# One TensorE run for a step's outputs, the next Gram products and the last transposes, in a scan with two feed-forward layers

## The chip, the cores and the metric

The kernel runs on one core of a Trainium2 chip. Its engines are TensorE (PE: matrix products and transposes; PEld is its loading of weights), VectorE (DVE), ScalarE (ACT), GpSimd (POOL) and SyncE (SP), whose queue issues most transfers (DMA). Each works through its own queue in order and waits at semaphores for the others. The metric is the device time of one execution in microseconds, as the median of several runs.

## What is computed

A chunked linear recurrence over 4 batches, 8 heads and 768 positions, then a normalisation and a gated layer, then a second layer with a squared ReLU:

```python
def _attn_ref(x, a, B, C):                 # head_dim 32, d_state 16
    log_a = np.log(np.clip(a, 1e-06, 1.0))
    for c in range(nc):                    # chunks of the sequence
        cum = np.cumsum(la, axis=-1)
        L = np.exp(cum[:, :, :, None] - cum[:, :, None, :]) * causal
        CB = np.einsum('bhin,bhjn->bhij', Cc, Bc)
        y_intra = np.einsum('bhij,bhjd->bhid', CB * L, xc)
        y_inter = np.einsum('bhin,bhnd->bhid', Cc, state) * np.exp(cum)[:, :, :, None]
        y[:, :, sl] = y_intra + y_inter
        state = decay_full[:, :, None, None] * state + np.sum(Bx, axis=2)

def _moe_ref(x, w_gate, w_val, w_out, rms_g):      # 3072 tokens, 256 -> 1536 -> 256
    xn = x / np.sqrt(np.mean(x * x, axis=-1, keepdims=True) + 1e-06) * rms_g
    g = xn @ w_gate
    return g * (1.0 / (1.0 + np.exp(-g))) * (xn @ w_val) @ w_out

def _moe2_ref(x, w_in, w_out, s, b):               # 256 -> 2048 -> 256
    r = np.maximum(x @ w_in, 0.0)
    return (s * (r * r) + b) @ w_out
```

## The kernel before

**The recurrence** is cut into 16 steps of 48 positions (counted from 0 here, as in the code). A step has two units, `c` and `c + 1`; each holds one chunk of two batches. In each step TensorE does three things for both units, all of them into the units' two PSUM tiles `y` (two banks each):

- `gram` (lines 549 to 565): 16 Gram products of B and C with a tile form of 32 rows by 64 columns (32*64 in the trace), read from `raw_bc`, which is loaded anew for each step by twelve transfers. From step 2 on this is the form used. DVE then multiplies them by the decays in `a_sb` to `m`, with four instructions.
- `outs` (586 to 617): 32 output products of `m` and `xh` in the form 64*64. `xh` holds the inputs of the chunk and, in 16 rows of each half, the state. ScalarE then copies the new state into the next step's `xh` (four copies), squares the rows for the norm and, after DVE (`ss`) and POOL (`rs`), scales them to `xn`.
- `turn` (637 to 658): 4 transposes of `xn`. ScalarE reads them from PSUM to `xth`, DVE writes the remainder to `xtl`. These are the columns of the first layer's input.

`scan` (495 to 504) comes before: it loads `a_sb` by two transfers (`load_a`), once the step before has used it, and a scan on DVE makes the decays.

**The layers** work on blocks of units, `BLOCKS = (4, 4, 4, 5, 5, 5, 5)`. For each of 12 hidden slices of a block, `hidden1` (774) has twelve products into the two banks `h`; ScalarE and DVE make `s`, `hi` and `lo` of them, and two slices later six products add to `o`. Each bank `h` is free for the next slice when ScalarE (first bank) and DVE (second bank, product `s`) have read it. The second layer follows when all steps are done, after some 322 us.

**What sets the order.** Nothing is issued where it is written. `Plan` records every instruction with its predecessors, plays the program through with costs of its own and issues all of it in the order that came out (line 370, which is why every row of the trace carries L370). The recorded order of the steps (`stream`, 661 to 669) sets what waits for what: an instruction that reads or overwrites a tile follows those recorded before it on that tile. `bundled` (507) makes the tile products of one kind and one step a group that the plan keeps together; `join` (131) gives the group's first instruction all waits of the others. Between the groups the plan puts products of the layers.

Of the kernel before, what the change touches and what calls it, by code (L numbers as in the profile page):

```python
# [8 lines left out]
F32 = mybir.dt.float32  # L9
# [10 lines left out]
P = 128  # L20
CH = 48
NST = 16
R = NST + CH
# [3 lines left out]
CPB = SEQ // CH  # L27
UT = 2 * CH
NPAIR = 2
NUNIT = CPB * NPAIR  # L30
NCLIP = 2 * NPAIR
FREE = 2 * NPAIR
SLOTS = NPAIR
AW = CH + 1
# [350 lines left out]
def scan_glu_relu2(ctx: ExitStack, tc: tile.TileContext, bc, xr, aa, cst, w1, w2, gn, sv, bv, out):  # L385
    nc = Plan(tc.nc)
# [19 lines left out]
    ps_y = ctx.enter_context(tc.tile_pool(name="ps_y", bufs=2, space=PS))  # L406
# [139 lines left out]
                            rhs=raw[:, 1:3, cols], start=True, stop=True, tile_position=(at, z * R),  # L546
                        )

    def gram(units):
        if units[0]:  # L550
            load_bc(units)
        for c in units:
            y_t[c] = ps_y.tile([P, 2, 512], F32, tag="y", name="y")
        bundled("g", units, gram_products, True)
        for c in units:
            g = gram_of(c)
            t = a_t.pop(c)
            m = att2.tile([P, NH, R], F32, tag="m", name="m")
            mv, tv = (v.rearrange("p (a b) r -> p a b r", a=2) for v in (m, t))
            nc.vector.tensor_tensor(out=mv[:, :, :, NST:R], in0=g[:, :, :, NST:R], in1=tv[:, :, :, 0:CH], op=ALU.mult)  # L560
            nc.vector.tensor_tensor(
                out=mv[:, :, :, 0:NST], in0=g[:, :, :, 0:NST],
                in1=tv[:, :, :, CH:AW].to_broadcast([P, 2, 4, NST]), op=ALU.mult,
            )
            m_t[c] = m
# [20 lines left out]
    def outs(units):  # L586
# [6 lines left out]
        if units[0] < FREE:  # L593
            nc.fresh = True
            for c in units:
                out_products([c])
                nc.fresh = True
        else:
            bundled("o", units, out_products, True)
        ss = att2.tile([P, NPAIR], F32, tag="ss", name="ss")  # L600
# [36 lines left out]
    def turn(units):  # L637
        for c in units:
            j = BLOCK[c]
            if c == FIRST[j]:  # L640
                xt_h[j] = xt_p.tile([P, 2, NB[j]], F32R if j else F32, tag="xth", name="xth")
                if j:
                    t = xt_p.tile([P, 2, NB[j]], F32R, tag="xtl", name="xtl")
                    xt_l[j] = [t[:, k] for k in range(2)]
        bundled("t", units, turn_products)
        for c in units:
            j, p = BLOCK[c], c % NPAIR
            step = steps_of(j, p).index(c // NPAIR)
            tp = y_t.pop(c)[:, 1, 4 * R:4 * R + 2 * P].rearrange("p (k z r) -> p k z r", k=2, z=2)
            src = [tp[:, k, :, NST:R] for k in range(2)]  # L650
            hi = [columns(xt_h[j][:, k], j, p)[:, step] for k in range(2)]
            for k in range(2):
                nc.scalar.activation(out=hi[k], in_=src[k], func=AF.Copy, scale=g_sb[:, k:k + 1])
            for k in range(2 if j else 0):
                lo = columns(xt_l[j][k], j, p)[:, step]
                nc.vector.scalar_tensor_tensor(
                    out=lo, in0=src[k], scalar=g_sb[:, k:k + 1], in1=f32(hi[k]), op0=ALU.mult, op1=ALU.subtract
                )


    def stream():
        s = []
        for c in range(0, NUNIT, NPAIR):
            units = range(c, c + NPAIR)
            s += [(6 * c + t, units, f) for t, f in zip((2, 4, 8), (scan, gram, outs))]
            apart = BLOCK[c] != BLOCK[c + 1]
            s += [(6 * c + 14, u, turn) for u in ([[c], [c + 1]] if apart else [units])]
        s.sort(key=lambda e: e[0])
        return [(units, f) for _, units, f in s]

# [494 lines left out]
```

## Time and profile before

| | |
|---|---|
| median of 3 runs | 630.87 us (630.2 to 632.45) |
| the profiled execution | 631.4 us |
| its span, first to last instruction | 629.4 us |
| TensorE busy | 619.1 us (98%) |
| VectorE busy | 481.7 us (77%) |
| ScalarE busy | 448.6 us (71%) |
| GpSimd busy | 49.4 us (8%) |
| granted TensorE clock | 0.999 of full speed |

The span stretches from the first to the last instruction of the program on any engine; the 2.0 us between it and the execution's time lie around it. A busy share is an average over stages. In a timeline of TensorE, a product starts before the one ahead of it has ended, since they are pipelined; the distance between two starts, not the duration of a row, tells what a product costs. An `xN` behind a row of the timeline counts trace records: each product of the small forms has two.

### The profile page before, as it was taken

What the parts mean: (1) busy time and instruction counts of PE and PEld (TensorE: products, weight loads), DVE (VectorE), ACT (ScalarE), POOL (GpSimd) and SP (SyncE); (2) the same over time, 40 slices, a digit from 0 to 9 for tenths busy, and PEclk for the clock granted to TensorE, in tenths of its full rate; (3) what the DMA queues carried; (4) which work ended last, traced back from release to release, by engine and by line L of the source; (5) the groups of instructions that cost most, each with busy time, mean ns of one, the idle gap of its engine ahead of it and who ended that gap; (6) DMA issues with size and microseconds to landing.
All of it is one profiled execution on the core that took longest, in us unless ns stands there. A gap on an engine that the chain in (4) does not pass through costs nothing.

```text
span 629.4 us, 12849 instructions
## 1 busy us (share of the span) xinstructions
PE 619.1 (98%) x4911; PEld 544.6 (87%) x4911; DVE 481.7 (77%) x972; ACT 448.6 (71%) x941; POOL 49.4 (8%) x88
## 2 busy tenths in 40 slices
PE   9899999999999999999999999999999999999996
PEld 7786899999888888888888889999999999999986
DVE  6999965778557656767774568798897897987976
ACT  5788635566545556664665579899898999998985
POOL 3000000001101111101232220000000000000000
PEclk9999999999999999999999999999999999999999
DMA  6877403344313433300200000001010010010101
GB/s 218 218 232 207 116 16 65 81 95 95 98 35 89 95 96 95 92 15 11 34 1 1 1 1 1 2 3 33 0 34 2 2 33 1 6 31 1 33 1 35
DMA packets 33694, 35.00 MB, mean 56 GB/s; under 512 B 14048, under 2 KB 30048, under 8 KB 33632
## 3 DMA queue, kind: packets, MB, share of 16 engines
q1 hardware_dynamic: 32688, 33.71, 20.7%
q8 instruction: 39, 0.64, 0.4%
q10 hardware_dynamic: 944, 0.46, 0.3%
q14 instruction: 23, 0.19, 0.1%
HBM read 30.90 MB, written 3.25 MB: 54 GB/s over the span
## 4 chain that ended last, share of the span: by engine, by line
PE 91%; DMA 2%; ACT 2%; DVE 2%; issue 1%; SPq 0%; DVEq 0%; ACTq 0%
PE h L370 52%; PE o L370 21%; PE acc L370 13%; PE y L370 5%; DMA a_sb<-a_scr 1%; DMA raw<-in_w 1%; PE o L363 1%; DVE a_sb L370 0%; ACT xth L370 0%; ACT e L370 0%; ACT xh L370 0%; DVE s L370 0%; ACT xn L370 0%; DVE m L370 0%; ACT sg L370 0%
## 5 line engine op out<-in xcount | busy, mean ns | idle before, releaser
L370 ACT CAST hi<-s 128x256 fp32r<-128x256 f32 (+2 forms) x170 | 80.1, 474 | 72.4 <-DVE s L370 69.9
L370 ACT ACTIVATE s<-h 128x512 f32<-128x512 f32 (+2 forms) x170 | 97.2, 572 | 36.1 <-PE h L370 33.1
L370 PE MATMUL h<-x1h,w2h 128*128 128x512 f32 x384 | 119.2, 391 | 0.0
L370 PE MATMUL h<-xth,w1h 128*128 128x480 f32 (+1 forms) x296 | 108.9, 371 | 1.4 <-DVE s L370 1.1
L370 PE MATMUL h<-xth,w1l 128*128 128x480 f32 (+1 forms) x296 | 109.3, 369 | 0.0
L370 PE MATMUL h<-xtl,w1h 128*128 128x480 f32 (+1 forms) x296 | 109.0, 370 | 0.0
L370 DVE TENSOR_TENSOR lo<-s,hi 128x256 fp32r<-128x256 f32 (+2 forms) x170 | 86.4, 509 | 28.1 <-ACT hi L370 25.4
L370 PE MATMUL acc<-hi,w2c 128*128 128x256 f32 x448 | 81.8, 281 | 0.0
L370 PEld LDWEIGHTS h<-x1h,w2h 128*128 128x128 f32 x384 | 69.2, 188 | 12.3
L370 DVE TENSOR_TENSOR s<-h,s 128x480 f32<-128x480 f32 (+1 forms) x74 | 45.6, 616 | 39.1 <-PE h L370 36.1
L370 PE MATMUL h<-x1l,w2h 128*128 128x512 f32 x192 | 75.0, 390 | 0.0
L370 PEld LDWEIGHTS acc<-hi,w2c 128*128 128x128 f32 x448 | 71.0, 189 | 2.3
L370 DVE TENSOR_TENSOR added<-s 128x256 f32<-128x256 f32 x144 | 56.5, 420 | 13.3 <-ACT s L370 12.3
L370 PEld LDWEIGHTS h<-xth,w1h 128*128 128x128 f32 x296 | 55.5, 188 | 9.8 <-DVE s L370 3.5
L370 PE MATMUL acc<-lo,w2c 128*128 128x256 f32 x224 | 63.1, 282 | 0.0
L370 ACT ACTIVATE s<-s 128x512 f32<-128x512 f32 x96 | 60.2, 633 | 1.9
L370 PEld LDWEIGHTS h<-xtl,w1h 128*128 128x128 f32 x296 | 55.5, 188 | 6.4 <-issue 1.2
L370 PEld LDWEIGHTS h<-xth,w1l 128*128 128x128 f32 x296 | 55.6, 188 | 6.1 <-issue 0.3
L370 PE MATMUL o<-hi,w1l 128*128 128x480 f32 (+1 forms) x148 | 54.3, 367 | 0.0
L370 PE MATMUL o<-lo,w1h 128*128 128x480 f32 (+1 forms) x148 | 54.0, 366 | 0.0
L370 PE MATMUL o<-hi,w1h 128*128 128x480 f32 (+1 forms) x148 | 53.9, 364 | 0.0
L370 DVE TENSOR_TENSOR lo<-added,hi 128x768 fp32r<-128x768 f32 x48 | 45.9, 956 | 0.5 <-ACT hi L370 0.5
(98 smaller groups left out, 1061.4 us busy)
## 6 DMA issues: line engine op xcount, KB each, us to landing
raw<-in_w SPq DMA_DIRECT2D x12, 768.0 KB
raw<-in_w SPq DMA_DIRECT2D x16, 512.0 KB, 3.9
a_sb<-a_scr SPq DMA_DIRECT2D x28, 196.0 KB, 4.4
xh<-in_xr SPq DMA_DIRECT2D x60, 48.0 KB, 1.9
raw_bc<-in_bc SPq DMA_DIRECT2D x56, 32.0 KB, 1.7
raw_bc<-in_bc SPq DMA_DIRECT2D x112, 16.0 KB, 3.3
out_t<-res SPq DMA_DIRECT2D x13, 96.0 KB, 2.0
out_t<-res SPq DMA_DIRECT2D x5, 144.0 KB, 1.9
```

The source lines that it names most:

```text
L363: self.nc.tensor.matmul(out=idle, lhsT=ones, rhs=ones, start=not fills, stop=True, skip_group_check=True)
L370: getattr(engine, op["fn"])(*op["args"], **op["kw"])
```

## The change

From step 5 to step 15, `outs` records one group in place of three: the transposes of the step before, the Gram products of the step after, and its own output products, in this order. `gram` and `turn` of these steps then record only what reads the results, and `turn` is recorded after the next step's `outs` (`late`), with the run's last product as a predecessor (`nc.after`). The transfers for the Gram products are recorded in `begin_gram`, ahead of the run. The two tiles `y` are made once (`y_p`) and serve all steps. Step 5's own Gram products stay a group of their own, as do the transposes of step 15; the run of step 15 has no Gram products.

```diff
+JOIN = (5, CPB - 1)
...
-    def gram(units):
+    y_p = [ps_y.tile([P, 2, 512], F32, tag="y", name="y") for _ in range(NPAIR)]
+
+    def joined(units):
+        return JOIN[0] <= units[0] // NPAIR <= JOIN[1]
+
+    def begin_gram(units):
         if units[0]:
             load_bc(units)
         for c in units:
-            y_t[c] = ps_y.tile([P, 2, 512], F32, tag="y", name="y")
-        bundled("g", units, gram_products, True)
+            y_t[c] = y_p[c % NPAIR]
+
+    def gram(units):
+        if not (units[0] and joined([units[0] - NPAIR])):
+            begin_gram(units)
+            bundled("g", units, gram_products, True)
...
+        elif joined(units):
+            ahead = range(units[0] + NPAIR, min(units[0] + 2 * NPAIR, NUNIT))
+            if ahead:
+                begin_gram(ahead)
+
+            def products(units):
+                for c in units:
+                    turn_products(c - NPAIR)
+                if ahead:
+                    gram_products(ahead)
+                out_products(units)
+            bundled("o", units, products, True)
         else:
             bundled("o", units, out_products, True)
...
-        bundled("t", units, turn_products)
+        if joined([units[0] + NPAIR]):
+            nc.after = nc.heads[f"o{units[0] // NPAIR * NPAIR + NPAIR}"][1]["i"]
+        else:
+            bundled("t", units, turn_products)
...
-            tp = y_t.pop(c)[:, 1, 4 * R:4 * R + 2 * P].rearrange("p (k z r) -> p k z r", k=2, z=2)
+            tp = y_p[c % NPAIR][:, 1, 4 * R:4 * R + 2 * P].rearrange("p (k z r) -> p k z r", k=2, z=2)
...
+        nc.after = None
...
-            s += [(6 * c + 14, u, turn) for u in ([[c], [c + 1]] if apart else [units])]
+            late = 6 * NPAIR + 8.5 if joined([c + NPAIR]) else 14
+            s += [(6 * c + late, u, turn) for u in ([[c], [c + 1]] if apart else [units])]
```

What the plan makes of it, on TensorE at the output products of step 8; `h` and `o` are products of the first layer. Before:

```order
L370 MATMUL h<-xth,w1h 128x384
L370 MATMUL h<-xth,w1l 128x384
L370 MATMUL y<-xh,m 64x32 x32
L370 MATMUL h<-xtl,w1h 128x384
L370 MATMUL o_399<-hi,w1h 128x384
```

and in the changed kernel (y<-ident,xn are the transposes of step 7, y<-raw_bc the Gram products of step 9):

```order
L371 MATMUL h<-xtl,w1h 128x384
L371 MATMUL h<-xth,w1h 128x384
L371 MATMUL y<-ident,xn 128x128 x4
L371 MATMUL y<-raw_bc 64x128 x16
L371 MATMUL y<-xh,m 64x32 x32
L371 MATMUL h<-xth,w1l 128x384
L371 MATMUL h<-xtl,w1h 128x384
```

Three places with layer products between them have become one; 43 layer products follow before the next such run.

On SP, the transfers of step 14. Before:

```order
L370 DMA xh<-in_xr 48x256 x4
L370 DMA raw_773<-in_w 128x512
L370 DMA raw_bc<-in_bc 32x2x128 x3
L370 DMA a_sb<-a_scr 64x2x392 x2
L370 DMA raw_bc<-in_bc 32x2x128
L370 DMA raw_bc<-in_bc 16x2x128 x8
```

and in the changed kernel:

```order
L371 DMA raw_bc<-in_bc 32x2x128 x4
L371 DMA raw_bc<-in_bc 16x2x128 x8
L371 DMA xh<-in_xr 48x256 x4
L371 DMA a_sb<-a_scr 64x2x392 x2
L371 DMA raw_bc<-in_bc 32x2x128 x4
```

The two loads of the decays, which stood among the twelve of the Gram inputs, now stand behind these and behind the inputs `xh`; the twelve of step 15 follow.

On DVE, around the scan of step 9 (`a_sb<-a_sb,delta`). Before:

```order
L370 TENSOR_SCALAR ss<-ss 128x2
L370 TENSOR_TENSOR lo<-s,hi 128x384
L370 SCALAR_TENSOR_TENSOR a_sb<-a_sb,delta 128x392 x2
L370 TENSOR_TENSOR s<-h,s 128x384
L370 TENSOR_TENSOR lo<-s,hi 128x384
L370 SCALAR_TENSOR_TENSOR xtl<-y,sb,xth 128x2x48 x2
```

and in the changed kernel:

```order
L371 SCALAR_TENSOR_TENSOR a_sb<-a_sb,delta 128x392
L371 TENSOR_SCALAR ss<-ss 128x2
L371 SCALAR_TENSOR_TENSOR a_sb<-a_sb,delta 128x392
L371 TENSOR_TENSOR s<-h,s 128x384
L371 SCALAR_TENSOR_TENSOR xtl<-y,sb,xth 128x2x48 x4
L371 TENSOR_TENSOR m<-y,a_sb 128x8x48 x2
L371 TENSOR_TENSOR m<-y,a_sb 128x8x16 x2
```

The scan is followed by the layer's `s` in both; `ss` of step 8, the remainders `xtl` of step 7 and the products `m` of step 9 now stand together around it.

## Rows read from the trace of the kernel before

**Rows 1.** the page's part 1 (busy us, share, instructions), and busy time of each engine by stretch:

```profile
PE 619.1 (98%) x4911; PEld 544.6 (87%) x4911; DVE 481.7 (77%) x972; ACT 448.6 (71%) x941; POOL 49.4 (8%) x88
...
85.00:325.00 240.00, 238.69 (x2226) 208.34 (x2225) 161.95 (x343) 136.46 (x340) 27.82 (x37) 1.00 0.28 66
```

**Rows 2.** TensorE's timeline at four transposes: start us, us, what it writes and reads, records:

```profile
198.99 0.38 PE L370 MATMUL h<-xth,w1l 128*128 128x480 f32 x1
199.21 0.60 PE L370 MATMUL y<-ident,xn 128*128 128x128 f32 x4
...
200.08 0.37 PE L370 MATMUL o<-hi,w1h 128*128 128x480 f32 x1
```

**Rows 3.** the same at the Gram products of one step:

```profile
202.24 0.38 PE L370 MATMUL h<-xth,w1l 128*128 128x480 f32 x1
...
202.89 0.38 PE L370 MATMUL h<-xth,w1l 128*128 128x480 f32 x1
203.20 0.69 PE L370 MATMUL y<-raw_bc 32*64 32x128 f32 x32
203.83 0.48 PE L370 MATMUL h<-xtl,w1h 128*128 128x480 f32 x1
...
204.36 0.37 PE L370 MATMUL h<-xth,w1l 128*128 128x480 f32 x1
```

**Rows 4.** the same at the output products of that step:

```profile
206.10 0.60 PE L370 MATMUL h<-xth,w1h 128*128 128x480 f32 x2
206.63 1.14 PE L370 MATMUL y<-xh,m 64*64 64x32 f32 x64
207.69 0.48 PE L370 MATMUL h<-xth,w1l 128*128 128x480 f32 x1
...
208.24 0.38 PE L370 MATMUL h<-xth,w1h 128*128 128x480 f32 x1
```

**Rows 5.** tile y by form: duration in ns min/median/max, first and last start:

```profile
L370 PE MATMUL y<-raw_bc x448: 267/268/319, 37.1 to 309.8; 32*64 32x128 f32 x150
```

**Rows 6.** TensorE's timeline early: eight ab products, then a full and a small form:

```profile
10.20 0.88 PE L370 MATMUL ab<-a_cl,ident 128*64 128x196 f32 x8
11.01 0.41 PE L363 MATMUL o<-const-bfloat16-1.0 128*128 128x128 bf16 x4
...
19.37 0.88 PE L370 MATMUL ab<-a_cl,ident 128*64 128x196 f32 x8
20.19 0.69 PE L370 MATMUL y<-first_bc 16*64 16x64 f32 x32
```

**Rows 7.** TensorE's waits of 85 to 325 us (total, times, longest us), and its timeline at the longest:

```profile
PE h L370 <- DVE s L370: 1.1, 3, 0.5
...
143.92 0.34 PE L370 MATMUL h<-xth,w1h 128*128 128x384 f32 x1
...
144.80 0.34 PE L370 MATMUL h<-xtl,w1h 128*128 128x384 f32 x1
145.57 0.44 PE L370 MATMUL h<-xth,w1h 128*128 128x384 f32 x1 [0.43 <-DVE s L370]
```

**Rows 8.** groups of instructions of 85 to 325 us: count, busy us, mean ns, idle before:

```profile
L370 DVE TENSOR_TENSOR_SCAN a_sb<-a_sb,delta 128x392 f32<-128x392 f32 x22 | 21.3, 987 | 15.3 <-DMA a_sb<-a_scr 13.4 <-DMA raw_bc<-in_bc 1.9
L370 DVE TENSOR_TENSOR m<-y,a_sb 128x384 f32<-128x384 f32 (+1 forms) x48 | 17.0, 415 | 2.4 <-PE y L370 2.4
L370 ACT COPY xh<-y 16x256 f32<-16x256 f32 x44 | 15.8, 359 | 0.6
```

**Rows 9.** DVE's timeline at the scan ahead of that wait:

```profile
144.09 0.97 DVE L370 TENSOR_TENSOR_SCAN a_sb<-a_sb,delta 128x392 f32<-128x392 f32 x1 [2.33 <-DMA a_sb<-a_scr]
```

**Rows 10.** SP's timeline: the a_sb loads of that scan, and the loads of a Gram input:

```profile
139.03 1.23 SPq L370 DMA_DIRECT2D a_sb<-a_scr  x2
...
189.72 1.75 SPq L370 DMA_DIRECT2D raw_bc<-in_bc  x4
...
192.84 4.94 SPq L370 DMA_DIRECT2D raw_bc<-in_bc  x8
```

## Prediction

> **What bounds the kernel.** First the page and its stretches [rows 1]: TensorE is busy 98% of the span, and in 85 to 325 us, where the steps that the change touches stand between the first layer's products, 238.7 of 240 us. Another engine's saving is worth nothing there; what counts is what TensorE spends on the attention and how long it waits. The timeline of TensorE then gives the price of an interruption. A product of width 480 follows the one before it every 0.217 us (202.24 to 202.89 is three of them) [rows 3]. Transposes: from the product at 198.99 to the one at 200.08 are 1.09 us, of which three ordinary products are 0.65, so the four transposes cost **0.44 us** [rows 2]. Gram products: 202.89 to 204.36 is 1.47 us less three products, **0.82 us** [rows 3]. In it 0.31 − 0.22 = 0.09 is lost on entry, 0.63 passes from the first Gram product to the next ordinary one, and that one and its successor take 0.53 instead of 0.43, 0.10 lost after it. Output products: 206.10 to 208.24 is 2.14 us less four products, **1.27 us** [rows 4]: about 0.10 on entry, 1.06 to the next ordinary product, 0.12 after it. A step thus pays 2.53 us in three interruptions.
>
> What TensorE waits for comes next. Between 85 and 325 us the view of its waits knows three on DVE's s, 1.1 us together, the longest half a microsecond (the timeline has 0.43 us of idle before 145.57) [rows 7]. Its cause stands on DVE: the scan at 144.09 came after 2.33 us of idling for the load of a_sb [rows 9], and the product s for which TensorE waits is queued behind the scan. The scans idled 13.4 us in all for that load [rows 8].
>
> **The joint.** Ten runs (steps 5 to 14, counted from 0) now hold the transposes of the step before, the Gram products of the step after and their own outputs; the run of step 15 has no Gram products, and transposes pay nothing for entry or exit (0.44 is four times their own 0.11), so joining them gains nothing. No product is removed: the same 4, 16 and 32 stand in each step. What can go is one exit and one entry, where Gram products meet output products.
>
> What that meeting costs is not in the trace, since the two are never neighbours there; both sides can be bounded. If TensorE must empty itself between two small forms as it does before an ordinary product, the Gram part keeps its 0.63 us and the joint saves only the 0.10 after it and the 0.09 to 0.10 before the outputs: 0.44 + 0.09 + 0.63 + 1.06 + 0.12 = 2.34 instead of 2.53, 0.19 a step, **1.9 us** over ten. If the output products follow without a gap, the Gram part shrinks to the distance of its first and last start, 0.69 us of the merged row less one product's 0.27 [rows 3, 5], and one beat, 0.44 us: 0.38 a step, 3.8 us. The nearest rows decide for the first: eight ab products (128*64) in front of an ordinary form take 11.01 − 10.20 = 0.81 us, in front of the 16*64 form 20.19 − 19.37 = 0.82 us [rows 6]. One small form followed by another costs as much as a small form followed by a full one. I take 1.9. Nothing excludes that the two small forms meet at a higher price; the bound on that side is that the joint saves nothing at all (below).
>
> The Trainium skill (TensorEngine Tiling, Key Properties) says that a change of tiling mode, not of the tile alone, drains TensorE; from 32*64 to 64*64 is such a change. By that rule the joint gains 1.9 us, and rows 6 agree with it.
>
> **What the run must wait for.** It starts when the latest of three things is there, and each wait sits in front of all ordinary products behind it. (a) The last step's normalised rows for the transposes and (b) the products m for the outputs: on TensorE the closest pairs of runs stand 43 products of width 384 apart, 43 × 0.176 = 7.6 us (0.176: 143.92 to 144.80 is five [rows 7]); there are six such close pairs (runs 5 and 6, 7 and 8, 8 and 9, 10 and 11, 12 and 13, 13 and 14), the others have 20 us and more. After a run ScalarE has four readers of the transposes, two squares, four copies of the state, 4 × 0.36 us [rows 8], and DVE four products m, 4 × 0.42 us [rows 8]; copies and m are 1.4 + 1.7 us, and with the six other readings put at the 0.36 us of a copy, 2.2 us, my estimate is that m is done some 5 us after the run, 2.5 us before it is due. (c) The inputs of the next Gram products. Their twelve loads may start once the Gram products in the run are over: four take SP 1.75 us, and eight 4.94 us although two a_sb loads stood in front and held a slot [rows 10]. That is 6.7 us of issuing; from the end of the Gram part to the next one lie 1.06 of outputs, 7.6 and 0.44, 9.1 us. The order of SP puts the a_sb loads behind these twelve, no longer between them, so the loads gain some of it; 2.4 us are left for the last landing. Both stay covered; if the cover goes, each microsecond is paid at each close pair.
>
> **The a_sb load.** This is the thinnest cover. It may be issued once m has read the tile, now after the run instead of right after the Gram products; from the first issue (139.03) to the scan (144.09) passed 5.1 us [rows 9, 10]. At a close pair: run ends, 5 us to m, 5.1 us to the scan: 10.1, while the next run ends at 7.6 + 2.3 = 9.9. Two scans of 0.99 us [rows 8] and s then stand on DVE where TensorE needs s only after 20 products, 3.5 us behind the run: 10.1 + 2.0 + 0.5 = 12.6 against 13.4. It holds by 0.8 us. In the kernel before the same queue failed three times for 1.1 us in all; the loads now run without the twelve others around them and the readers of a step come in one burst. I take half of the 1.1 as gone, 0.55 us; the bounds are all of it gone, and what the third rival gives.
>
> The rest costs nothing that I can find. The transposes of a step are read later, after the run's outputs (1.7 us), but the order gives the first products of a new block 8 to 12 others ahead of them (1.4 us and more), and the run that closes a block stands within some 15 products of where its transposes stood alone. Readers issued after the run do not enter it, so no instruction of the run waits for one. The two PSUM tiles held throughout are the same two buffers as before. Before 85 us and after 325 us TensorE's order is the same but for single pieces.
>
> **Sum.** The profiled execution took 631.4 us (629.4 between first and last instruction); the median of the three runs is 630.87, 0.5 lower, and the sum is made as a difference and taken off the median: 1.9 + 0.55 = 2.45, **628.4 us**.
>
> **Rivals.**
> 1. Seamless joint: 3.8 + 0.55, **626.5 us**. For it: inside a run products of one form start some 14 ns apart (0.42 us for 32 records) although they change their place in the array each time. Against it: rows 6. The Trainium skill (TensorE: Matmul & The Clock Gate, Part 3, The mechanism) has weight loads for another row group pulled ahead of running products, by which the meeting would be seamless.
> 2. The joint does not do what it is for: a meeting of two small forms costs a full exit and a full entry, and each part keeps its 0.44, 0.82 and 1.27 us. Only the waits could move: 630.87 less 0.3, **630.6 us**. For it: rows 6, read strictly, show a second small form never cheaper than a full one. Against it: the 0.10 after an exit falls on ordinary products, and two of them fewer are hit.
> 3. Slower: the a_sb load decides at the close pairs. If it lands over 0.8 us later than reckoned, DVE's queue (scan, ss, scan, s) holds TensorE. From 0.4 us of waiting a pair the gain is eaten (six pairs, 2.45 us); at 0.8 us a pair, more than the longest wait seen, 4.8 us are paid against 1.9 gained, 630.87 + 2.9, **633.8 us**. For it: scans already idle 13.4 us for this load. Against it: the margin above, and that 13.4 us of idling [rows 8] led to 1.1 us of waits [rows 7].
>
> **Chances.** Forecast 0.48, seamless 0.18, nothing spared 0.21, slower 0.13. A measurement of this kernel can tell about 0.3%, 1.9 us: faster means below 629.0. Three quarters of the forecast's own spread (stalls between 0.5 worse and all gone, 1.4 to 3.2) and the seamless case lie there: 0.36 + 0.18 + 0.01 = 0.55. Within 0.3%: 0.12 + 0.20 + 0.01 = 0.33. Slower: 0.12. The range of 8 in 10 goes from 626.1 (most of the seamless case) to 631.6 (nothing spared with a little lost).
>
> **What would show it.** Right: in TensorE's timeline a run from the product before the transposes to the second product behind the outputs costs about 2.34 us beyond the ordinary ones, with about 0.63 us from first Gram product to first output product; waits on s of TensorE between 85 and 325 us at or under 1.1 us. Seamless: 0.44 us in that place. Nothing spared: output products more than 1.06 us long inside a run, or the run at 2.5 us. Slower: idle of TensorE before h released by DVE s, six times and longer than 0.5 us, each with a scan idle for a_sb in front. I am wrong altogether if the span changes before 85 or after 325 us, or if a run itself waits for its loads.

## The result, and the profile after

The changed kernel is slower: a median of 634.46 us (20 runs, 632.43 to 637.76) against 631.17 us before (20 runs), a ratio of 1.0054 with a 95% interval of 1.0037 to 1.0070. Forecast were 628.4 us and a range that ended at 631.6. The profiled execution took 633.45 us, with a span of 631.7 us (before 631.4 and 629.4). Of a kernel below, a_again, three of twelve executions took 759 us and more; its median is 630.80 us without them and 631.95 us with them, the figure that some expectations quote.

The page's part 1 after, and its stretches (columns as in [rows 1]):

```profile
PE 619.5 (98%) x4910; PEld 548.3 (87%) x4910; DVE 483.4 (77%) x972; ACT 447.3 (71%) x941; POOL 52.5 (8%) x88
...
0.00:85.00 85.00, 81.21 (x867) 67.25 (x868) 76.67 (x146) 57.44 (x122) 8.90 (x29) 0.98 0.64 183
85.00:325.00 240.00, 238.05 (x2236) 211.40 (x2235) 166.58 (x350) 137.07 (x345) 31.40 (x38) 1.00 0.27 66
```

TensorE was busy 0.6 us less of the middle than before (238.05 of 240 against 238.69), although it had less to do there; and the granted clock up to 85 us was 0.98. The page's part 4, the chain of work that ended last:

```profile
PE 83%; DVE 7%; DMA 6%; SPq 2%; issue 1%; ACT 0%; DVEq 0%
```

Before, TensorE had 91% of that chain, DMA and DVE 2% each. The load of first_bc is new in it with 2%, and that of a_sb has 3% instead of 1%. Where they stand is seen when the same products are set against each other by their start times in both traces: the first layer's products come 2.57 us later from 27 to 75 us; over the middle the lag falls to 1.19 us and stays so through the second layer; after the last product another 1.08 us go until the end. 2.57 − 1.38 + 1.08 = 2.27 us, the difference of the spans.

**The start.** TensorE's timeline after, from the first transposes:

```profile
13.55 0.76 PE L371 MATMUL y<-ident,xn 128*128 128x128 f32 x4
14.15 0.51 PE L364 MATMUL o<-const-bfloat16-1.0 128*128 128x128 bf16 x6
16.28 0.29 PE L371 MATMUL y<-first_bc 16*64 16x64 f32 x2 [1.62 <-DMA first_bc<-in_bc]
17.00 0.67 PE L371 MATMUL y<-first_bc 16*64 16x64 f32 x14 [0.43 <-ACT xth L371]
17.61 2.91 PE L371 MATMUL h<-xth,w1f 128*128 128x192 f32 x8
20.45 1.22 PE L371 MATMUL y<-first_bc 16*64 16x64 f32 x32
```

and before:

```profile
13.81 0.60 PE L370 MATMUL y<-ident,xn 128*128 128x128 f32 x4
14.26 0.75 PE L363 MATMUL o<-const-bfloat16-1.0 128*128 128x128 bf16 x10
15.13 1.71 PE L370 MATMUL h<-xth,w1f 128*128 128x192 f32 x8
16.76 0.69 PE L370 MATMUL y<-first_bc 16*64 16x64 f32 x32
```

Eight Gram products of step 1 (16 records) now stand ahead of the first four products of the first layer. They wait 1.62 us for their load and 0.43 us for ScalarE's readers, and the layer's products stand behind them. ScalarE is held too: the second two of its four readers of the transposes start at 16.61 us, after 1.54 us of waiting for the first of these Gram products, and the layer's products need what they write. The layer's four products then take 2.91 us in place of 1.71, and the clock says why (stretches of 2 us; the third number from the end is the granted clock):

```profile
14.00:16.00 2.00, 0.66 (x8) 0.47 (x8) 0.49 (x2) 1.06 (x3) 0.00 (x0) 1.00 0.22 43
16.00:18.00 2.00, 1.29 (x17) 1.12 (x18) 1.97 (x4) 1.39 (x4) 0.00 (x0) 0.91 0.74 151
18.00:20.00 2.00, 2.00 (x8) 2.00 (x7) 0.96 (x1) 0.80 (x2) 0.00 (x0) 0.50 0.97 312
20.00:22.00 2.00, 2.00 (x41) 1.50 (x41) 1.08 (x3) 0.61 (x2) 0.00 (x0) 0.73 0.83 116
```

After the idling between 14 and 18 us it fell from 2.4 to 1.2 GHz, 0.50, until some 21 us. Before, it was 1.00 in the same stretches.

**The joined run** is what was forecast. The timeline of that of step 10, the step to which [rows 4] belong:

```profile
204.90 0.38 PE L371 MATMUL h<-xtl,w1h 128*128 128x480 f32 x1
205.12 0.60 PE L371 MATMUL y<-ident,xn 128*128 128x128 f32 x4
205.65 0.69 PE L371 MATMUL y<-raw_bc 32*64 32x128 f32 x32
206.27 1.13 PE L371 MATMUL y<-xh,m 64*64 64x32 f32 x64
207.34 0.48 PE L371 MATMUL h<-xth,w1h 128*128 128x480 f32 x1
207.66 0.38 PE L371 MATMUL h<-xth,w1l 128*128 128x480 f32 x1
```

It takes 2.22 us from the first transpose to the next ordinary product, and 0.10 more behind that, 2.32 in all. From the first Gram product to the first output product pass 0.62 us, as to an ordinary product in [rows 3].

**The waits** of TensorE between 85 and 325 us, which were 1.1 us in three places [rows 7]:

```profile
PE h L371 <- DVE s L371: 1.8, 2, 1.7
```

The longest is at a close pair of runs (those of steps 8 and 9), behind the second. TensorE:

```profile
171.49 0.38 PE L371 MATMUL h<-xtl,w1h 128*128 128x480 f32 x1
173.54 0.48 PE L371 MATMUL h<-xth,w1h 128*128 128x480 f32 x1 [1.67 <-DVE s L371]
```

SP ahead of it:

```profile
154.58 6.84 SPq L371 DMA_DIRECT2D raw_bc<-in_bc  x12
161.53 1.75 SPq L371 DMA_DIRECT2D xh<-in_xr  x4
163.37 1.23 SPq L371 DMA_DIRECT2D a_sb<-a_scr  x2
```

and DVE:

```profile
169.25 0.97 DVE L371 TENSOR_TENSOR_SCAN a_sb<-a_sb,delta 128x392 f32<-128x392 f32 x1 [2.24 <-DMA a_sb<-a_scr]
170.14 0.53 DVE L371 TENSOR_TENSOR lo<-s,hi 128x384 fp32r<-128x384 f32 x1
170.60 0.16 DVE L371 TENSOR_SCALAR ss<-ss 128x2 f32<-128x2 f32 x1
170.67 0.97 DVE L371 TENSOR_TENSOR_SCAN a_sb<-a_sb,delta 128x392 f32<-128x392 f32 x1
171.55 0.40 DVE L371 TENSOR_SCALAR e<-raw 128x512 uint16<-128x512 uint16 x1
171.87 0.31 DVE L371 SCALAR_TENSOR_TENSOR xtl<-y,sb,xth 128x96 fp32r<-128x96 f32 x1
172.61 0.32 DVE L371 SCALAR_TENSOR_TENSOR xtl<-y,sb,xth 128x96 fp32r<-128x96 f32 x1 [0.43 <-ACT xh L371]
172.84 0.65 DVE L371 TENSOR_TENSOR s<-h,s 128x480 f32<-128x480 f32 x1
```

The loads went out when SP had issued the twelve of the Gram inputs and four of xh. The scan stood 5.9 us behind the issue and held DVE for 2.24 us, and s, for which TensorE waited, stood seven instructions behind it.

### The profile page after: what moved, and what is told of

It is laid out like the page before. It is cut to its first block, busy times and chain, and to the rows that moved or that the text cites. A ratio compares the mean times of both kernels' runs of the same rounds, so it can differ in the third digit from the quotient of the medians.

```text
span 631.7 us, 12836 instructions
## 1 busy us (share of the span) xinstructions
PE 619.5 (98%) x4910; PEld 548.3 (87%) x4910; DVE 483.4 (77%) x972; ACT 447.3 (71%) x941; POOL 52.5 (8%) x88
## 4 chain that ended last, share of the span: by engine, by line
PE 83%; DVE 7%; DMA 6%; SPq 2%; issue 1%; ACT 0%; DVEq 0%
PE h L371 47%; PE o L371 19%; PE acc L371 13%; PE y L371 4%; DMA a_sb<-a_scr 3%; SPq L371 2%; DMA first_bc<-in_bc 2%; DVE w1f L371 1%; DVE a_sb L371 1%; DVE e L371 1%; DVE m L371 1%; DVE h L371 1%; DVE s L371 1%; DVE raw L371 1%; DVE xtl L371 0%
## 5 line engine op out<-in xcount | busy, mean ns | idle before, releaser
L371 ACT ACTIVATE s<-h 128x512 f32<-128x512 f32 (+2 forms) x170 | 97.2, 572 | 35.8 <-PE h L371 32.4
```

The source lines that it names most:

```text
L371: getattr(engine, op["fn"])(*op["args"], **op["kw"])
```

## The experiments

One execution tells little of waits that depend on when a transfer lands, so the table sets the middle of all traces side by side. It is worked out from the start times of TensorE's products: the stretch from the 41st record of the first layer's products with w1f (at 32 to 41 us) to the first product of the second layer; in it the time that the tile products take, with what is lost at their entries and exits up to two products behind them ("runs"); and gaps of over 40 ns elsewhere, from 85 us on ("waits", which includes slower products right behind a gap). The last column is the median and its ratio to the kernel before, run beside it on the same chip; only the ratio can be compared between rows, since the kernels ran on different chips, and the median of before lay between 630.1 and 632.6 us.

| kernel | stretch | runs | waits | time, ratio (95%) |
|---|---|---|---|---|
| before | 336.0 | 35.9 | 2.1 | 631.17 |
| before_again | 334.8 | 36.1 | 0.8 | 0.9996 (0.9972 to 1.0021) |
| b_held_only | 334.7 | 36.1 | 0.6 | 634.47, 1.0066 (1.0043 to 1.0089) |
| changed | 334.6 | 33.4 | 3.1 | 634.46, 1.0054 (1.0037 to 1.0070) |
| e_fill_wait | 335.3 | 33.4 | 3.7 | 632.40, 1.0044 (1.0018 to 1.0069) |
| a_early_fresh | 334.5 | 33.4 | 2.9 | 631.44, 1.0015 (0.9993 to 1.0038) |
| a_again | 336.8 | 33.4 | 5.4 | 630.80, 1.0007 (0.9979 to 1.0035) |
| t_turn_apart | 335.0 | 35.9 | 1.1 | 630.44, 0.9987 (0.9967 to 1.0007) |
| h1_a_on_pool | 333.5 | 34.0 | 1.3 | 629.85, 0.9987 (0.9968 to 1.0005) |
| g1_a_on_act | 334.7 | 34.1 | 2.5 | 629.41, 0.9984 (0.9963 to 1.0005) |
| g1_again | 333.0 | 34.1 | 0.8 | 630.01, 0.9992 (0.9972 to 1.0012) |
| hb_before_a_on_pool | 335.5 | 35.4 | 2.0 | 633.14, 1.0038 (1.0018 to 1.0057) |
| c2_plan_knows | 332.9 | 33.3 | 1.0 | 629.25, 0.9952 (0.9934 to 0.9969) |

The traced execution is the slowest of its kernel's for b_held_only (637.31 us), e_fill_wait (639.36), g1_a_on_act (634.51) and c2_plan_knows (632.56): a trace shows what happens, the medians how much of it is usual.

**The early order.** b_held_only makes the two tiles once, as the change does, and joins nothing:

```diff
-JOIN = (5, CPB - 1)
+JOIN = (99, 99)
```

> The two PSUM tiles y are made once, as in the changed kernel, but no run is joined (JOIN lies outside the steps). Against the kernel before, TensorE's order differs in one place: eight Gram products of step 1 stand ahead of the first four first-layer products, where before all sixteen of that half stood behind them. Theory 1 (the early order): this alone costs 2.6 us, as the two traces stand apart at 24 us, so 633.8 us against 631.2, and the offset of the first layer's products stays 2.5 to 2.7 us to the end. Theory 2 (the joined runs are what costs; the early offset is luck of one profiled execution): no difference from before within 0.5 us.

It came to 634.47 us, 1.0066: slower than before by 2.7 to 5.6 us, as much as the whole change, with nothing joined. In its trace the clock stayed at 0.50 from 17 to 31 us after a wait of 1.74 us, and the first layer's products were 7.4 us later than in the trace of before from 25 us on.

a_early_fresh is the opposite, the change with tiles made anew for steps 0 to 4:

```diff
         for c in units:
+            if c // NPAIR < JOIN[0]:
+                y_p[c % NPAIR] = ps_y.tile([P, 2, 512], F32, tag="y", name="y")
             y_t[c] = y_p[c % NPAIR]
```

> The changed kernel with new tiles y for steps 0 to 4, shared ones only from step 5 on. Its order differs from the changed kernel's in the same eight Gram products of step 1 alone (and one ScalarE piece beside them); all joined runs are the same. Theory 1 (the early order costs 2.6, the joint saves 2.1, waits cost 1.3): the offset at 24 us is 0, and the median is 634.5 - 2.6 = 631.9 us, or 630.8 if the later end of the last stores (1.1 us) was chance. Theory 2 (the joined runs cost): 634 us as in the changed kernel.

631.44 us, 1.0015 in place of 1.0054: by these ratios some 2.5 us of the loss are gone, with eight Gram products put back. Theory 1 is right, and that the kept tile moved them is shown. Why it did is read from the plan's code and was not tested by itself: with a new tile for each step, step 1's Gram products waited for everything done to the old tile, the readers of its transposes among it; with one tile for all steps the plan keeps this dependency by PSUM bank, and half of them could be set earlier.

e_fill_wait asks whether it is the wait or the clock:

```diff
+            if op["eng"] == "tensor" and getattr(op["kw"].get("lhsT"), "name", "").startswith("first_bc"):
+                bc_seen += 1
+                for _ in range(34 if bc_seen == 33 else 0):
+                    self.nc.tensor.matmul(out=idle, lhsT=ones, rhs=ones, start=False, stop=True, skip_group_check=True)
```

> The changed kernel with 34 more of the small bf16 filler products put ahead of the eight early Gram products, where TensorE waits 1.62 us for the load of first_bc; nothing else. Theory 1a (half of the early 2.6 us is the granted clock that falls to 0.5 after that wait): the clock stays 1.00 from 16 to 24 us, the first eight first-layer products take 1.7 us instead of 2.9, and the offset at 24 us falls from 2.6 to about 1.4; median 633.3. Theory 1b (all of it is the waiting, and the clock would have been hidden): the offset stays 2.3 to 2.6 us.

The median of 632.4 us lies 2 us under that of the changed kernel, but the ratios to before, 1.0044 and 1.0054, overlap: the time doesn't decide it. The trace does in part. Its two stretches after the fillers:

```profile
22.00:24.00 2.00, 1.57 (x25) 1.33 (x24) 0.42 (x1) 0.47 (x3) 0.00 (x0) 1.00 0.72 194
24.00:26.00 2.00, 2.00 (x22) 1.73 (x22) 0.00 (x0) 1.70 (x3) 0.00 (x0) 1.00 0.51 208
```

The clock stayed at 1.00, and the eight records that took 2.91 us took 1.57. Since executions differ in where the first transposes stand (13.8, 17.4 and in this one 20.2 us, whatever the kernel), I count from there to the 41st record of the first layer's products: 19.6 and 18.1 us in the two traces of before, 18.5 and 18.1 with new early tiles, 22.4 in the changed kernel, 27.0 in b_held_only, 21.1 with the fillers. In these traces the clock thus costs about one of the 3 to 4 us in the changed kernel, and six in b_held_only; the rest, 1.5 to 3 us, is the place in the queue. That split is rough: the fillers took 2.16 us, whether or not the load was still out by then. Over the executions the clock matters less. The five of the changed kernel with a mean granted clock of 0.998 or more have a median of 634.08 us, the eleven with 0.995 or less one of 634.42; of b_held_only four at 0.998 or more have 634.07 and four at 0.992 or less 634.77. So most of the usual loss is there at the full clock.

**The joint and its waits.** Without the early loss the joined kernel should have been 2 us faster than before, and it was not. Both kernels were run and profiled again, with no edit:

> The kernel before, profiled a second time: how much of a trace's differences is the execution and not the order. From the 20 times of before (two heaps, about 629.4 and 632.2 us) I expect the stretch up to 27 us to move by 1 to 3 us between two executions, and the stretch from the first to the last step of the first layer (85 to 325 us) by under 0.7 us, since its waits are 1.1 us in all. If the middle moves by more, the waits on a_sb are luck of the execution and a single trace can't size them.

> The kernel with new tiles for steps 0 to 4 and the joined runs, a second time. Theory 1 (the joint saves 2.1 us, its waits cost some 0.5 to 1 more than before's): the stretch from 85 to 325 us is again 1 to 2 us shorter than in before, and the median is 1 to 2 us under before's. Theory 2 (the saving is eaten by waits that one trace doesn't show): the stretch is within 0.5 us of before's or longer, and the median is 0.5 to 1 us over before's, as in the first twelve runs (631.4 against 630.1).

The runs cost 33.4 us in the four joined traces so far and 35.9 to 36.1 in the three unjoined ones: the joint's gain does not vary. The waits do: 2.1, 0.8 and 0.6 us unjoined, 3.1, 3.7, 2.9 and 5.4 joined, means of 1.2 and 3.8. Theory 2 fits: 2.6 us gained, 2.6 us given back, and ratios whose intervals hold 1. The groups of the scan in the two joined traces (a_early_fresh, then a_again):

```profile
L371 DVE TENSOR_TENSOR_SCAN a_sb<-a_sb,delta 128x392 f32<-128x392 f32 x22 | 21.0, 967 | 15.4 <-DMA a_sb<-a_scr 15.4
```

```profile
L371 DVE TENSOR_TENSOR_SCAN a_sb<-a_sb,delta 128x392 f32<-128x392 f32 x22 | 21.7, 998 | 16.8 <-DMA a_sb<-a_scr 16.8
```

Against 13.4 us in [rows 8]. Two things could be changed: when the load goes out, or where the scan stands. In the traces of before, m ended 1.8 to 2.8 us after a step's last Gram product and the loads went out 2.2 to 3.3 us after it; joined, m ended 1.8 to 13.8 us after it, at most runs 7 to 10, and the loads went out 6 to 14 us after it, up to 5.4 us behind m.

**When the load goes out.** The first attempt doubles a_sb (the load's output gets the same slots, and delta is held in bf16 to make room):

```diff
-SLOTS = NPAIR
+SLOTS = 2 * NPAIR
-            a_t[c] = a_sb[:, c % NPAIR]
+            a_t[c] = a_sb[:, c % SLOTS]
```

> The same as the kernel with new early tiles, and a_sb twice as large (four units in place of two; delta in bf16 to make room), so that a step's decays are loaded while the step before still uses its own. Theory 1 (the scan's load is what TensorE's waits on s come from): scans no longer idle for a_sb, TensorE's waits on s between 85 and 325 us fall from about 3.0 us to under 0.5, and the time is 2 to 2.5 us under the kernel with new early tiles: 629 to 629.9. Rival (the waits come from DVE's own queue, xtl and s behind the scans, and the load is only the last named): waits stay at 2 to 3 us, and the time stays within 0.7 us of that kernel.

631.74 us, 1.0016, waits of 2.5 us: the rival's outcome, though not a test of it. The loads still went out 6.8 to 11.8 us after the last Gram product, no earlier than with one tile, and the scans still idled 10.2 us for them, so that Theory 1 was not tried. Two kernels with these loads on ScalarE's queue, the second without joined runs:

```diff
-                nc.sync.dma_start(
+                nc.scalar.dma_start(
                     out=a_sb[z * R:(z + 1) * R, units[0] % SLOTS:units[0] % SLOTS + NPAIR].rearrange("p s h r -> p s (h r)"),
...
-JOIN = (5, CPB - 1)
+JOIN = (99, 99)
```

> As the kernel with a_sb twice as large, but its two loads per step are issued by ScalarE's queue, so that they no longer stand on SP behind Gram inputs that wait for their tile. If the waits on s come from the late landing of a_sb: scans idle under 2 us in all (before 13.4), waits on s between 85 and 325 us fall under 0.4 us, and the time is about 2 us under the kernel with new early tiles. If they come from the burst behind a joined run (xtl, copies of xh and m take turns on DVE and ScalarE, with s behind them): waits stay between 0.8 and 2 us and the time within 0.7 us of that kernel.

> As the last one (a_sb twice as large, loaded by ScalarE's queue), but without any joined run: three interruptions a step as before. Against the last kernel it shows the joint alone, with a_sb out of the way in both. Joint as predicted (1.9 to 2.1 us over ten runs): this kernel is 1.5 to 2.1 us slower than the last one. Joint eaten by the burst of readers behind it: within 0.5 us, and its waits on s under 0.4 us where the last one's stay near 1 to 2.

634.56 us (1.0052) and 632.49 us (1.0028). Both lost at the start, since the doubled tile moved the early order too (3.6 and 3.5 us of gaps before 85 us in place of 1.0), so their times say nothing of the middle. Their runs cost 33.7 and 35.8 us, the joint again; their waits were 4.3 us (one of 2.2 on s, and products at a clock of 0.50 behind it) and 0.2 us. The joined kernel waited and the other did not, with the same loads on the same queue; so in these two traces, one of each, another queue alone did not free the joined one.

Then one a_sb as in the change, with only the loads from step 6 on moved, so that the start is that of a_early_fresh (g1 has nc.scalar in the same place; hb is the kernel before with the first edit; for GpSimd's loads the plan gets one more queue):

```diff
-                nc.sync.dma_start(
+                queue = nc.gpsimd if units[0] >= 6 * NPAIR else nc.sync
+                queue.dma_start(
```

> The kernel with new tiles for steps 0 to 4 and the joined runs; from step 6 on the two loads of a_sb are issued by GpSimd's queue. There each goes out when m has read the tile, and not when SP is through with the twelve loads of the Gram inputs and xh, which stand ahead of it. In the two traces of that kernel m ended 7.1 to 10.2 us after a run's last Gram product and the load went out up to 5.4 us after m. Theory 1 (SP's queue makes the load late, the late scan holds s): issue within 0.4 us of m's end, TensorE's waits after 85 us fall from 2.9 and 5.4 us to under 1.5 us, the joined runs still cost 33.4 us, and the median is 1.5 to 2.5 us under that kernel's 631.4 to 631.9. Theory 2 (m itself is late, and the burst of readers behind a run is what holds s): waits stay above 2.5 us, the time within 0.7 us.

> The same with ScalarE's queue in place of GpSimd's. Theory 1: waits after 85 us under 1.5 us as with GpSimd, less what ScalarE now loses by standing at the load until m is done (m ends just before it is due, so up to 1 us a step on ScalarE, and some of it on s). Theory 2: waits above 2.5 us as in the kernel without it.

> The joined kernel with new early tiles and a_sb on ScalarE's queue, a second time: how far the waits of one execution differ from the next one's, and whether it is faster than before. If the first trace (2.5 us of waits after 85 us) was at the upper end, waits are now 0.5 to 2 us; the median 1.5 to 2.5 us under before's, ratio 0.996 to 0.9985.

> The kernel before, with the loads of a_sb on GpSimd's queue from step 6 on, and nothing joined. Its waits after 85 us were 2.1 and 0.8 us in two traces. If the load's place on SP is what they come from, they fall under 0.5 us and the median by 0.3 to 1.5 us; if the load is late for another reason, they stay. Against the joined kernel with the same loads it gives the joint alone: 2.5 us by the runs' cost on TensorE.

From step 6 on the loads went out 0.3 to 0.4 us (GpSimd) and 0.03 us (ScalarE) after m. The waits fell to 1.3, 2.5 and 0.8 us, a mean of 1.5. The ratios to before, 0.9984 to 0.9992, lie 1 to 2 us under those of a_early_fresh and a_again, but hold 1 in their intervals and overlap theirs: the traces say that SP's queue is part of the waits, the times do not decide it. In each of the three traces one run now waited for its own Gram inputs, 0.3 to 0.4 us, and cost 3.0 to 3.15 us in place of 2.32, which is why their runs add up to 34.0 and 34.1. hb_before_a_on_pool was a miss: 1.0038, slower, with waits of 2.0 us. Its loads went out 2.1 to 2.8 us after the last Gram product instead of 2.2 to 3.3, so there was little to gain; its trace shows 1.35 us more at the start, with TensorE's order still that of before: the clock was at 0.50 from some 21 to 25 us, after a wait of 1.11 us at 18 to 19 us. That does not say why all its runs should be slower, which stays open.

Four kernels combined both, from step 6 on: slots in turn with GpSimd's queue and with ScalarE's, and two tiles in turn with ScalarE's queue and with SP.

```diff
+    def slot(units):
+        return NPAIR if units[0] >= 6 * NPAIR and units[0] // NPAIR % 2 == 0 else 0
-            a_t[c] = a_sb[:, c % NPAIR]
+            a_t[c] = a_sb[:, slot(units) + c % NPAIR]
...
+    a_two = [const.tile([P, SLOTS, NH, AW], F32, name=f"a_sb{k}") for k in range(2)]
     def load_a(units):
+        a_sb = a_two[units[0] >= 6 * NPAIR and units[0] // NPAIR % 2 == 0]
```

> New tiles for steps 0 to 4, joined runs, a_sb loads on GpSimd's queue from step 6 on, and from step 6 on two halves of a_sb in turn (delta in bf16 to make room), so that the load waits neither for SP nor for the m of the step before. Theory 1 (both together are what made the scan late): loads go out more than 5 us earlier against m, TensorE's waits after 85 us are under 0.6 us (1.25 with GpSimd's queue alone), and the median is 0.5 to 1 us under that kernel's, about 629. Theory 2 (what is left of the waits is the burst of readers behind a run): waits stay between 1 and 2.5 us and the median within 0.5 us of it.

> The same with ScalarE's queue. ScalarE no longer stands at the load until m is done (2.5 us of waits with its queue and one a_sb). Theory 1: waits after 85 us under 0.6 us, and the median about that of the kernel on GpSimd's queue. Theory 2: waits stay over 1 us.

> In the two kernels with a doubled a_sb the loads still went out 0.03 us (ScalarE) and 0.3 us (GpSimd) behind the last m of the step before: the dependency is kept for the whole tile, so doubling the tile did not free them. Here the two halves are two tiles, used in turn from step 6 on; the order on TensorE and on the queues is that of the kernel with the doubled a_sb on ScalarE's queue. Theory 1 (the late load is what holds s): loads go out before m ends, scans idle for a_sb under 3 us (5.8), waits after 85 us under 0.5 us (0.96), and the median is 0.5 us or more under that kernel's 630.9. Theory 2 (the rest are readers in a burst): waits stay at 0.8 to 1.2 us.

> The same two tiles, but the loads stay on SP. The wait for m is gone, SP's order behind the twelve Gram loads is not. If the wait for m is most of the late load: waits after 85 us under 1.2 us, as with another queue. If SP's order is: waits stay at 2.5 us and more, as in the joined kernel with new early tiles (2.9 and 5.4).

631.38 (0.9999), 630.88 (1.0004), 631.22 (1.0001) and 632.42 us (1.0018), waits of 1.5, 1.0, 1.3 and 5.7: no better than one tile on another queue, and on SP as bad as ever. What the expectation of w3_two_tiles_act says of w1 and w2, that the tile is tracked as a whole, is not borne out: in w3, too, with two tiles, each load from ScalarE's queue but the first stood 0.03 us behind the last m that ended. The plan had used the room to set the scans a step ahead, ahead of the m of the step before, so that the load still followed the m that frees its tile. More room for the load moved the scan forward with it.

**The burst of readers.** t_turn_apart leaves the transposes a group of their own:

```diff
-                for c in units:
-                    turn_products(c - NPAIR)
                 if ahead:
...
-            late = 6 * NPAIR + 8.5 if joined([c + NPAIR]) else 14
-            s += [(6 * c + late, u, turn) for u in ([[c], [c + 1]] if apart else [units])]
+            s += [(6 * c + 14, u, turn) for u in ([[c], [c + 1]] if apart else [units])]
```

> The kernel with new early tiles, but only the next Gram products and the outputs share a run; the four transposes stay a group of their own, at the place that the kernel before gave them, and so their readers xth and xtl no longer fall together with the readers of the outputs. TensorE: the runs of the middle cost 33.4 us or up to 1 us less, since the transposes lose nothing at entry and exit (0.44 alone, 0.53 inside a run). If the burst of readers is what delays m and s: copies of xh no longer wait for xtl (3.4 and 4.4 us in the two traces with joined transposes, to under 0.5), waits after 85 us fall under 1.5 us, and the median is 1.5 to 2.5 us under 631.4 to 631.9. If the late load of a_sb alone does it: waits stay at 2.5 to 5 us.

630.44 us, 0.9987. The copies of xh no longer waited for xtl (0.5 us in place of 3.4 and 4.4), and the waits on s fell to 0.6 us. But TensorE now waited inside runs:

```profile
PE y L371 <- DVE xtl L371: 1.2, 2, 0.8
PE h L371 <- DVE s L371: 0.6, 1, 0.6
```

Three runs with such waits at their entry or inside (1.4, 1.0 and 0.2 us) make up its 35.9 us against 33.4; so the transposes' place made no difference to the joint itself. The burst is a part of the loss by the waits on s, and the ratio came out about where moving the load had brought it, again with 1 in its interval (0.9967 to 1.0007).

**Where the scan stands.** The last experiment moves no load. It takes a_early_fresh and lets the plan reckon with 1.5 us more between an a_sb load and what reads it:

```diff
+            if o["fn"] == "dma_start" and str(o["kw"]["out"].name).startswith("a_sb"):
+                lag += 1.5
             op["preds"][o["i"]] = lag + (self.DMA_TAIL if o["fn"] == "dma_start" else 0.0)
```

> The joined kernel with new early tiles, loads of a_sb on SP and one tile as there; only the plan reckons with 1.5 us more until an a_sb load has landed. (Between issue and scan the traces have 5 to 6.5 us.) The plan then sets the scans further back in DVE's order, with s ahead of them. If a scan that stands too early in DVE's order, and stops it until the load lands, is what holds s: scans idle under 8 us for a_sb (15.4 and 16.8), waits after 85 us fall from 2.9 and 5.4 us to under 1.5 us although no load goes out earlier, and the median is 1 to 2 us under 631.4 to 631.9. If the load must come earlier: waits stay above 2.5 us, or turn into waits of the runs on m.

629.25 us against 632.62 on the same chip, 0.9952 (0.9934 to 0.9969): faster than the kernel before beside it by 2 to 4 us. But 632.62 is the highest median that before had beside any kernel here, and 629.25 is not clear of the 629.41 to 630.01 us of the kernels with the loads on another queue; how much of the ratio is the scan's place stays open. The loads went out no earlier, 7.4 to 11.4 us after the last Gram product. The scans' group:

```profile
L373 DVE TENSOR_TENSOR_SCAN a_sb<-a_sb,delta 128x392 f32<-128x392 f32 x22 | 21.1, 975 | 4.0 <-DMA a_sb<-a_scr 4.0
```

4.0 us of idling in place of 15.4 and 16.8, and waits of 1.0 us. DVE at the same step as above, its loads issued at 163.80:

```profile
170.84 0.66 DVE L373 TENSOR_TENSOR s<-h,s 128x480 f32<-128x480 f32 x1 [1.48 <-PE h L373]
171.73 0.32 DVE L373 SCALAR_TENSOR_TENSOR xtl<-y,sb,xth 128x96 fp32r<-128x96 f32 x1 [0.23 <-ACT xn L373]
171.96 0.96 DVE L373 TENSOR_TENSOR_SCAN a_sb<-a_sb,delta 128x392 f32<-128x392 f32 x1
```

s now waits for TensorE, not TensorE for s, and the scan behind it, 8.2 us after the issue, waits for nothing. So it is enough to move the scan: the waits can go although the load is as late as before. A scan that stands in DVE's order before its load has landed, with s behind it, is thus at least a large part of what ate the joint's gain. It is not isolated: the longer lag changed the plan's order elsewhere too, in some 40 places on TensorE and some 70 on DVE. And idling of the scans alone does not size the waits: in w4_two_tiles_sp they idled 11.9 us for a_sb and TensorE waited 5.7, in the kernel before 13.4 and 2.1.

## Why the prediction was wrong

**The joint: right.** Forecast were 2.34 us for a run and 0.63 us from the first Gram product to the first output product; measured were 2.32 and 0.62. Unjoined, the three places take 0.44 + 0.82 + 1.27 = 2.53 us, so a run saves 0.21, ten of them 2.1 us, against 1.9 forecast; the rest of the 2.6 in the table are short waits that the table counts with the unjoined groups, such as 0.41 us at the transposes at 113.5 us in the trace of before. The first rival, the seamless joint, would have shown 0.44, and the second no gain: both are out. The Trainium skill (TensorEngine Tiling (Array Packing), Key Properties) has TensorE drain when the tiling mode changes. These traces agree, with 0.62 us at the meeting of two small forms and 0.63 at that of a small and a full one. What the Trainium skill says of weight loads for other row groups, that they go ahead of running products (TensorE: Matmul & The Clock Gate, Part 3, The mechanism), did not make the meeting seamless here.

**The start: the step that failed.** "Before 85 us and after 325 us TensorE's order is the same but for single pieces", and "The two PSUM tiles held throughout are the same two buffers as before". Both are so, and I took both to cost nothing. The single piece was eight products ahead of the first product of a layer, at a place where their load had not landed; its price is 2.7 to 5.6 us by b_held_only against before, and some 2.5 to 3 us by the ratios of the changed kernel and of a_early_fresh and a_again. I had marked an early shift as what would prove me wrong altogether, and did not price the one early move that the order showed.

**The a_sb load: right place, wrong sign.** I named it the thinnest cover and then booked half of the stalls as gone, 0.55 us. In the runs the waits grew by 2.6 us instead. The reckoning, "10.1 + 2.0 + 0.5 = 12.6 against 13.4", failed in two terms. m was put 5 us behind a run; it ended 7 to 10 us after the last Gram product at most runs, and that product is 1.3 us ahead of a run's end. And the load was put right behind m; at 163.37 it stood behind sixteen others on SP, twelve for the Gram inputs (6.84 us) and four for xh (1.75 us). The first I had summed, as 6.7 us, for the Gram inputs and not for the load queued after them, the second nowhere. The burst of readers, which I counted in favour, put copies of xh behind xtl and xtl behind the scan. This is the third rival, and that its 633.8 us came near the result is luck. Its mechanism gave 2.6 us in one to three places, not 0.8 at each of six pairs, and by itself it only ate the gain (a_early_fresh and a_again, 1.0015 and 1.0007); what made the kernel slower was the start.

**The end: not seen.** The last stores were issued at the same distance from the last product as before (0.90 to 2.21 us), but SP's last wait for them stands 5.7 us behind that product in the changed kernel and 4.6 in before; a_again has 5.8, before_again 4.6, and g1_a_on_act and t_turn_apart, joined as well, have 4.8 and 4.6. So 1.1 us of the result are there, and it is not the joint as such; what makes the same stores land later is open.

**The sum** by what was measured: about 3 for the start, nothing for joint and waits together, 1.1 at the end, some 4 us against the 3.3 us of the medians, whose interval is 2.3 to 4.4.

## What to carry to other kernels

Where a planner sets the order, a change of a tile's lifetime is a change of its dependencies everywhere, and the first microseconds, in which every load is still on its way, are where moved instructions cost most here, some 3 us for eight products: price each move there, however small. A saving on the bound engine is worth nothing while an instruction that waits for a transfer stands ahead of its feeder in an in-order queue; before moving the transfer, look whether the waiting instruction can stand later. And one trace does not size waits on transfers: two traces of the same kernel had 2.9 and 5.4 us.

## What the runs showed of the hardware

- TensorE's clock fell to 0.50 after idling of 1.6 to 1.7 and 0.4 us close together at 14 to 17 us, and stayed there for 3 us in one trace and 14 us in another; with 34 small fillers in the gap it stayed at 1.00 in the one trace taken. Between executions at a mean granted clock of 0.998 and more and those at 0.995 and less, the medians differ by 0.3 us (the changed kernel) and 0.7 us (b_held_only).
- From the issue of the two a_sb loads (196 KB each) to their scan pass mostly 4.9 to 6.1 us, on any of three queues (SP's, ScalarE's, GpSimd's).
- Four transposes ahead of Gram products start 0.53 us before them, ahead of an ordinary product 0.35, with 0.08 lost right behind. So 0.53 is the 0.44 of the transposes alone and the 0.09 of a small form's entry: joining them neither gains nor loses.
- The last stores of the program, equal in size and order of issue, took 1.1 us longer to land in the changed kernel, although its orders on TensorE, VectorE and ScalarE are those of before from 335 us on.
